# DMA transposes in place of TensorE transposes, chunks of 128 and 97 rows, and warming matmuls, in an attention plus Fourier-mix plus feed-forward kernel

## The chip, the cores and the metric

One core of one Trainium2 chip. The time is device microseconds of a whole launch; lower is better. The kernel before took 689.9 us (median of three runs, 689.3 to 690.1). Engines: PE is TensorE, DVE VectorE, ACT ScalarE, POOL GpSimd, SP the engine that issues most DMAs here. The kernel's matmuls write to PSUM tiles (`psS`, `psF`, `psT`); the copy out of one by VectorE or ScalarE is called its evacuation.

## The reference

Eight batches of 448 rows, 12 heads of 64, width 768:

```
attn  = relu(q @ k^T / 8)^2 / 448
x     = heads_to_rows(attn @ v)                     # (8, 448, 768)
u     = x + real(fft(fft(x, axis=1), axis=2))
un    = (u - mean(u)) / sqrt(var(u) + 1e-6)         # per row
out   = u + relu(un @ w1) @ w2                      # w1 768x3072, w2 3072x768
```

The two Fourier transforms are matmuls with cosine and sine tables ("mix"). By symmetry only half of the rows is computed, and the lower half comes out mirrored.

Of the kernel before, what the change touches and what calls it, by code (L numbers as in the profile page):

```python
# [9 lines left out]
FP32 = mybir.dt.float32  # L10
# [32 lines left out]
class Streams:  # L43
# [8 lines left out]
    def dma(self, start, nbytes):  # L52
        self.dma_free = max(self.dma_free, start + 1.0) + nbytes / 400e3
        return self.dma_free + 1.2
# [60 lines left out]
def kernel(  # L115
# [14 lines left out]
    R1 = R + 1  # L130
    NS = S // 2 + 1
    NQ = 2 * NS
# [6 lines left out]
    SC = [(0, R), (R, NS)]  # L139
    XB = 2  # L140
# [8 lines left out]
    HS = S // 2  # L149
    utop = [dram.tile([HS, D], FP32, name=f"utop{b}") for b in range(B)]  # L150
    ubot = [dram.tile([HS + 1, D], FP32, name=f"ubot{b}") for b in range(B)]

# [19 lines left out]
    rev = const.tile([128, R], BF16, name="rev")  # L172

    back = [const.tile([R, 1], mybir.dt.int32, name=f"back{i}") for i in range(2)]
    qT_bufs = []
# [5 lines left out]
    def dft_indices():  # L181
        nc.gpsimd.iota(drow[:, 0:2], pattern=[[R, 2]], base=0, channel_multiplier=1,
                       allow_small_or_imprecise_dtypes=True)
        nc.gpsimd.iota(drow[:, 4:7], pattern=[[128, 3]], base=0, channel_multiplier=1,
                       allow_small_or_imprecise_dtypes=True)
        nc.gpsimd.iota(dcol[:, 0:NS], pattern=[[1, NS]], base=0, channel_multiplier=0,
                       allow_small_or_imprecise_dtypes=True)
        nc.gpsimd.iota(dcol2, pattern=[[1, 2], [2, KH]], base=0, channel_multiplier=0,
                       allow_small_or_imprecise_dtypes=True)

    def small_constants():
        nc.vector.memset(zero_t, 0.0)
        nc.vector.memset(eps_t, 1e-6)
        for i in range(3):
            t = const.tile([128, NQ], BF16, name=f"qT{i}")
            nc.vector.memset(t[:, NS:NS + 1], 0.0)
            nc.vector.memset(t[:, NQ - 1:NQ], 0.0)
            qT_bufs.append(t)

    def mirrors():  # L200
        nc.gpsimd.memset(rev, 0.0)
        nc.gpsimd.affine_select(out=rev, in_=rev, compare_op=ALU.not_equal, fill=1.0,
                                base=1 - R, pattern=[[1, R]], channel_multiplier=1)
        for i in range(2):
            nc.gpsimd.iota(back[i], pattern=[[0, 1]], base=(2 - i) * R, channel_multiplier=-1)

    seq = const.tile([R1, 2, 2, NS], BF16, name="seqm")
# [3 lines left out]
    def build_dft():  # L211
# [16 lines left out]
        for t in range(2):  # L228
            e = yield need("DVE", 0.5)
            y = work.tile([128, 4 * KH], FP32, name="dfty", tag="u", bufs=2)  # L230
            for i in range(2):
                nc.vector.tensor_scalar(y[:R1, i * NS:(i + 1) * NS], col[:R1, 0:NS],
                                        row[:R1, i:i + 1], 0.25 if t == 0 else 0.0,
                                        op0=ALU.mult, op1=ALU.add)
            yield from sincos(seq[:, t, :, :].rearrange("p a s -> p (a s)"), y, 2 * NS, R1)
# [17 lines left out]
    BQ = [Bufs(3) for _ in range(3)]  # L253

    def load_group(i):
# [3 lines left out]
        for x, (nm, src) in enumerate((("q", q), ("k", k), ("v", v))):  # L259
            e = yield need("POOL", 0.85, bufs=[BQ[x]])  # L260
            t = work.tile([R, 2 * HG, 2 * Dh], BF16, name=f"{nm}n", tag=f"{nm}n", bufs=3)
# [3 lines left out]
            ready[i][x].t = sch.dma(e, GRP)  # L265
# [7 lines left out]
            if i == 1 and x == 2:  # L273
                yield need("POOL", 0.7)
                mirrors()

# [39 lines left out]
    xTs, As, Bs = [[] for _ in range(B)], [[] for _ in range(B)], [[] for _ in range(B)]  # L316
# [4 lines left out]
    BQR, BQT, BKT = Bufs(2), Bufs(3), Bufs(2)  # L321
    turned = [[None] * MC for _ in range(B)]
    turned_at = [[Cell() for _ in range(MC)] for _ in range(B)]

    def turning():
        for b in range(B):
            for m in range(MC):
                g, h0 = divmod(2 * m, HG)
                if h0 == 0:

                    qk = []
                    for x in range(2):
                        e = yield need("DVE", 0.42, [ready[b * NG + g][x]], [BQR] if x == 0 else [])
                        o = work.tile([R, 4, HG, Dh], BF16, name="qkr", tag=f"qkr{x}", bufs=2)
                        nc.vector.tensor_copy(o, loads[b * NG + g][x])  # L335
                        BQ[x].free.append(e)
                        qk.append(o.rearrange("p c h d -> p c (h d)"))

                hs = slice(h0 * Dh, (h0 + 2) * Dh)
                early = b == 0  # L340
                e = yield need("PE", 8 * 0.055, [e + LATENCY["DVE"]], [BF if early else BT])
                pt = psF(BF16) if early else psT(BF16)
                for c in range(4):
                    for x in range(2):
                        nc.tensor.transpose(pt[:, x * S + c * R:x * S + (c + 1) * R],  # L345
                                            qk[x][:, c, hs], ident[:R, :R])
                if h0 > 0:
                    BQR.free.append(e)
                e1 = yield need("DVE", 0.85, [e + LATENCY["PE"]], [BQT])
                qT = qT_bufs[(b * MC + m) % 3]  # L350

                nc.vector.tensor_copy(qT[:, 0:2 * R].rearrange("p (r j) -> p r j", j=2),  # L352
                                      pt[:, 0:2 * R].rearrange("p (j r) -> p r j", j=2))
                nc.vector.tensor_copy(qT[:, NS + 1:NS + 2 * R - 1].rearrange("p (r j) -> p r j", j=2),
                                      pt[:, 2 * R:4 * R].rearrange("p (j r) -> p r j", j=2)[:, :0:-1, ::-1])

                nc.vector.tensor_copy(qT[:, 2 * R:4 * R + 1:2 * R], pt[:, 2 * R:4 * R:R])
                e2 = yield need("ACT", act(S), [e + LATENCY["PE"]], [BKT])
                kT = work.tile([128, S], BF16, name="kT", tag="kT", bufs=2)
                nc.scalar.activation(kT, pt[:, S:2 * S], AF.Copy)  # L360
                (BF if early else BT).free.append(max(e1, e2))
                turned[b][m] = qT, kT
                turned_at[b][m].t = max(e1, e2) + LATENCY["ACT"]

    def attention(b):
# [4 lines left out]
        for p in range(NP + 2):  # L370
            m, c0 = divmod(p * G, 4)
            deps, bufs, dur = [], [], 0.0
            if p < NP:
                deps.append(turned_at[b][m])
                bufs += [BS] * G
                dur += G * mm(NQ) + SWITCH
            if p >= 2:
# [6 lines left out]
                dur += G * mm(NQ) + SWITCH  # L384
# [3 lines left out]
            if p < NP:  # L388
                qT, kT = turned[b][m]
                for c in range(c0, c0 + G):  # L390
                    sc = psS()
                    for h in range(2):
                        ps = slice(h * Dh, (h + 1) * Dh)
                        nc.tensor.matmul(sc[:R, h, 0:NQ], lhsT=kT[ps, c * R:(c + 1) * R], rhs=qT[ps, :],  # L394
                                         start=True, stop=True)
                    scs.append(sc)
                if c0 + G == 4:
                    BQT.free.append(e)
                    BKT.free.append(e)
            av_end = None  # L400
            if p >= 2:
# [3 lines left out]
                for c in range(ca, ca + G):  # L405
                    sq = sqs.pop(4 * ma + c)[0]
                    for h in range(2):
                        nc.tensor.matmul(av[h * Dh:(h + 1) * Dh, 0:NQ], lhsT=vn[:, c, h0 + h, :],  # L408
# [7 lines left out]
            for i in sorted(relus):  # L416
                r, t = relus.pop(i)
                e1 = yield need("DVE", dve2(2 * NQ), [t], [BSQ])
                sq = work.tile([R, 2, NQ], BF16, name="sq", tag="sq", bufs=4)
# [3 lines left out]
            for i, sc in enumerate(scs):  # L423
                e1 = yield need("ACT", act(2 * NQ) - 0.03, [e - dur * 0.5 + LATENCY["PE"]], [BAR])
                r = work.tile([R, 2, NQ], BF16, name="rsc", tag="rsc", bufs=2)
                nc.scalar.activation(r, sc[:R, :, 0:NQ], AF.Relu)  # L426
                BS.free.append(e1 + 0.1)
                relus[p * G + i] = (r, e1 + LATENCY["ACT"])
            if av_end is not None:
                m2 = ma  # L430
                e1 = yield need("DVE", dve(NQ) + 2 * dve2(NS), [av_end],
                                [BX[m2]] + ([BA[m2]] if m2 < 3 else []))
                x = work.tile([128, NQ], BF16, name="xT", tag=f"xT{m2}", bufs=1)
                nc.vector.tensor_scalar(x, av[:, 0:NQ], 1.0 / (64.0 * S), None, op0=ALU.mult)  # L434
                BT.free.append(e1 - 2 * dve2(NS))
                xTs[b].append(x)
                x_ready[b][m2].t = e1
                f = work.tile([128, 2, NS], BF16, name="fold", tag=f"fold{min(m2, 3)}", bufs=1)
                nc.vector.tensor_tensor(f[:, 0, :], x[:, 0:NS], x[:, NS:NQ], op=ALU.add)
                nc.vector.tensor_tensor(f[:, 1, :], x[:, 0:NS], x[:, NS:NQ], op=ALU.subtract)  # L440
                F.append(f)
                if m2 >= 3:
                    i = m2 - 3
                    e1 = yield need("DVE", 2 * dve2(NQ))
                    t = work.tile([128, 2, NS], BF16, name="diff", tag=f"diff{i}", bufs=1)
                    nc.vector.tensor_tensor(t, F[i], f, op=ALU.subtract)
                    Bs[b].append(t)
                    nc.vector.tensor_tensor(F[i], F[i], f, op=ALU.add)
                    As[b].append(F[i])
                    ab_ready[b][i].t = e1 + LATENCY["DVE"]  # L450
# [5 lines left out]
    BXN = [Bufs(XB), Bufs(XB)]  # L456
# [4 lines left out]
    u_stored = [[Cell() for _ in range(4)] for _ in range(B)]  # L461
    un_ready = [[Cell() for _ in range(2)] for _ in range(B)]
    uns = [[None] * 4 for _ in range(B)]
    groups, tails = [], []

    def mix_rows(b, ch, pcs):
# [3 lines left out]
        xT = xTs[b]  # L470
        xs = []
        for i in range(2):

            e = yield need("PE", 6 * 0.06, x_ready[b], [BT])
            px = psT(BF16)
            c0 = i * NS + s0
            for m in range(MC):
# [288 lines left out]
```

## The kernel before: what the change touches

The feed-forward of a pair of batches is cut into one group of 384 rows (feed-forwards 0, 2, 4, 6; "even") and one of 512 rows (1, 3, 5, 7; "odd"); feed-forwards are numbered from 0 here. While feed-forward *b* runs, TensorE does, in gaps chosen by a list scheduler in the program, attention of the next two batches and the mix of batch *b+1*. The scheduler fixes the order of instructions on every engine when the kernel is built; on the chip each engine then takes them in that order. One constant says how early attention may run, in units of one feed-forward:

```python
    LEAD = 1.6
    ...
            lead = b + p / NP - LEAD        # p: step of the attention of batch b
            e = yield need("PE", dur + SWITCH, deps, bufs, lambda: progress[0] >= lead)
```

All transposes are matmuls against an identity. Queries and keys (q/k):

```python
                    for x in range(2):
                        nc.tensor.transpose(pt[:, x * S + c * R:x * S + (c + 1) * R],
                                            qk[x][:, c, hs], ident[:R, :R])
                # ... three VectorE copies build qT, one ScalarE copy builds kT
```

The attention result is made as x^T and turned back into rows for `u`, six transposes for each of four row blocks; then the rows are normalised on VectorE, and `un` is turned for the feed-forward:

```python
            for m in range(MC):
                nc.tensor.transpose(px[:n, m * 128:(m + 1) * 128], xT[m][:, c0:c0 + n], ident)
            nc.scalar.activation(x[:n], px[:n, 0:D], AF.Copy)
            # ... mix, u, statistics ...
            nc.vector.tensor_scalar(un[:n], u[:n], rstd[:n, i:i + 1], nmr[:n, i:i + 1],
                                    op0=ALU.mult, op1=ALU.add)
            # ... per 256 columns:
                    nc.tensor.matmul(pu[:, h, c0:c0 + w], lhsT=uns[b][t][:n, ms], rhs=idn, ...)
            nc.scalar.activation(dst[...], pu[:, :, c0:c1], AF.Copy)     # unT
```

## Time and profile before

| | before |
|---|---|
| span of the profiled run | 686.8 us |
| first feed-forward matmul | 90.14 us |
| third to fifth feed-forward (two batches) | 155.40 us |
| TensorE busy in those two batches | 153.74 us |

The third row is the yardstick. The first matmul of each feed-forward is easy to find in the timeline of TensorE (the first one that reads `unT` after the last that reads `hT`), and from the third to the fifth (2 to 4) the kernel is in its steady rhythm: one group of 384 and one of 512 rows, with attention and mix of two batches in between. Here it is as a line of the windows table of the kernel before (stretch in us, its length, then busy time and number of instructions of PE, PEld, DVE, ACT and POOL, granted clock, DMA share, GB/s):

```profile
249.79:405.19 155.40, 153.74 (x1069) 83.76 (x1072) 94.25 (x219) 86.47 (x137) 28.11 (x31) 1.00 0.44 80
```

TensorE idles 1.66 us in 155.40. What is taken from TensorE here can be gained; a new wait of TensorE is paid in full.

### The profile page before, as it was taken

How to read it: one execution, taken by the hardware profiler on the slowest of the kernel's cores; microseconds unless marked ns; L12 is line 12 of the kernel's file. 1: busy time of each engine (PE TensorE's matmuls, PEld its weight loads, DVE VectorE, ACT ScalarE, POOL GpSimd, SP SyncE). 2: the span in 40 equal slices, each digit the busy share in tenths (PEclk: the TensorE clock that was granted, in tenths of full speed). 3: DMA queues.
4: the chain of work that ended last, by engine and by line, in shares of the span. 5: the costliest groups of instructions: out<-in, count | busy, mean ns of one | idle time of the engine just before them, and what ended most of it. 6: DMA issues, size and time to landing. Idle time of an engine off the chain costs nothing.

```text
span 686.8 us, 10715 instructions
## 1 busy us (share of the span) xinstructions
PE 640.7 (93%) x4270; PEld 347.9 (51%) x4288; DVE 388.1 (57%) x902; ACT 354.9 (52%) x556; POOL 126.3 (18%) x154
## 2 busy tenths in 40 slices
PE   2777399999999999999999999999999999999997
PEld 1235245654447545664446545664446545664464
DVE  7765956396545865396545964386545944280011
ACT  3755377527655466526755467426755367414400
POOL 8313321131112211131102111122101200030000
PEclk9999589999999999999999999999999999999999
DMA  9996994436315464435325464435232420042011
GB/s 125 212 167 109 225 151 41 41 130 125 32 17 94 141 110 42 41 130 118 34 20 82 154 111 42 41 129 111 26 36 41 150 89 1 1 151 69 1 70 69
DMA packets 82178, 59.70 MB, mean 87 GB/s; under 512 B 67528, under 2 KB 70600, under 8 KB 82128
## 3 DMA queue, kind: packets, MB, share of 16 engines
q0 software_dynamic: 71808, 31.46, 34.5%
q1 hardware_dynamic: 10320, 27.56, 12.1%
q8 instruction: 33, 0.54, 0.3%
q14 instruction: 17, 0.14, 0.1%
HBM read 62.91 MB, written 22.04 MB: 124 GB/s over the span
## 4 chain that ended last, share of the span: by engine, by line
PE 67%; DVE 19%; ACT 5%; DMA 4%; issue 2%; POOL 2%; ACTq 0%; DVEq 0%; POOLq 0%
PE psF L678 32%; PE psF L713 18%; PE psT L408 5%; PE psS L394 5%; DVE stats L522 4%; ACT rsc L426 3%; DVE un L536 3%; PE psS L573 3%; DVE sq L420 2%; DVE o L695 2%; PE psT L345 2%; DMA kn<-in_k_dram 2%; DMA w<-in_moe_w_ch_dram 2%; DVE u L512 2%; PE psT L478 1%
## 5 line engine op out<-in xcount | busy, mean ns | idle before, releaser
L426 ACT ACTIVATE rsc<-psS 112x900 bf16<-112x900 f32 x192 | 174.6, 921 | 132.9 <-PE psS L394 72.7
L678 PE MATMUL psF<-unT,w 128*128 128x384 bf16 (+1 forms) x1134 | 231.5, 354 | 2.5 <-ACT hT L668 1.4
L713 PE MATMUL psF<-w,hT 128*128 128x384 bf16 x1344 | 231.6, 326 | 0.0
L713 PEld LDWEIGHTS <-hT 128*128 128x128 bf16 x1344 | 127.0, 98 | 91.9 <-issue 14.0
L678 PEld LDWEIGHTS <-w 128*128 128x128 bf16 x1152 | 107.6, 98 | 113.7 <-issue 23.3
L668 ACT ACTIVATE hT<-psF 128x384 bf16<-128x384 f32 (+1 forms) x192 | 104.2, 545 | 61.1 <-PE psF L678 60.9
L420 DVE TENSOR_TENSOR sq<-rsc 112x900 bf16<-112x900 bf16 x192 | 114.0, 621 | 37.8 <-ACT rsc L426 35.7
L394 PE MATMUL psS<-qT,kT 64*112 64x450 bf16 x384 | 67.6, 413 | 14.1 <-ACT rsc L426 7.3
L695 DVE TENSOR_TENSOR o<-psF,o 128x384 f32<-128x384 f32 x56 | 30.7, 548 | 76.8 <-PE psF L713 76.7
L408 PE MATMUL psT<-sq,vn 112*64 112x450 bf16 x384 | 63.1, 398 | 11.1 <-DVE sq L420 10.7
L434 DVE TENSOR_SCALAR xT<-psT 128x450 bf16<-128x450 f32 x48 | 30.0, 625 | 75.5 <-PE psT L408 75.3
L262 POOL DMA_DIRECT2D vn<-in_v_dram x24 | 20.9, 871 | 268.0 <-PE psT L408 267.0
L394 PEld LDWEIGHTS <-kT 64*112 64x112 bf16 x384 | 21.9, 132 | 50.3 <-issue 43.9
L352 DVE COPY qT<-psT 128x224 bf16<-128x224 bf16 x42 | 16.4, 391 | 49.7 <-PE psT L345 49.3
L511 POOL TENSOR_TENSOR u<-tp,xn 112x385 f32<-112x385 f32 (+1 forms) x16 | 14.9, 934 | 149.6 <-DVE tp L502 128.6
L408 PEld LDWEIGHTS <-vn 112*64 112x64 bf16 x384 | 16.3, 111 | 47.3 <-issue 44.4
L345 PEld LDWEIGHTS <-qkr 112*128 112x128 bf16 x384 | 25.5, 107 | 18.0 <-DVE qkr L335 11.6
L522 DVE BATCH_NORM_STATS2 stats<-u 112x6 f32<-112x384 f32 (+1 forms) x64 | 31.6, 534 | 0.0
L526 ACT ACTIVATE std<-mv,eps_t 112x2 f32<-112x2 f32 (+1 forms) x16 | 4.7, 296 | 50.5 <-DVE mv L523 50.5
L536 DVE TENSOR_SCALAR un<-u,rstd,nmr 112x768 bf16<-112x768 f32 (+1 forms) x32 | 28.3, 915 | 0.6
L484 ACT ACTIVATE xn<-psT 112x768 bf16<-112x768 bf16 (+1 forms) x32 | 25.3, 812 | 6.5 <-PE psT L478 6.5
L586 DVE CAST pc<-psS 112x384 bf16<-112x384 f32 (+1 forms) x16 | 9.5, 594 | 32.0 <-ACT pc L584 32.0
(72 smaller groups left out, 498.1 us busy)
## 6 DMA issues: line engine op xcount, KB each, us to landing
out_dram<-o SPq DMA_DIRECT2D x28, 384.0 KB
qn<-in_q_dram POOLq DMA_DIRECT2D x24, 224.0 KB, 5.3
kn<-in_k_dram POOLq DMA_DIRECT2D x24, 224.0 KB, 5.8
vn<-in_v_dram POOLq DMA_DIRECT2D x24, 224.0 KB, 4.3
utop<-u SPq DMA_DIRECT2D x16, 336.0 KB
w<-in_moe_w_ch_dram POOLq DMA_DIRECT2D x12, 384.0 KB, 13.7
w<-in_moe_w_ch_dram POOLq DMA_DIRECT2D x4, 1152.0 KB, 17.7
o<-utop SPq DMA_DIRECT2D x8, 384.0 KB
```

What stands on the lines that cost most here:

```text
L345: nc.tensor.transpose(pt[:, x * S + c * R:x * S + (c + 1) * R], qk[x][:, c, hs], ident[:R, :R])
L394: nc.tensor.matmul(sc[:R, h, 0:NQ], lhsT=kT[ps, c * R:(c + 1) * R], rhs=qT[ps, :], start=True, stop=True)
L408: nc.tensor.matmul(av[h * Dh:(h + 1) * Dh, 0:NQ], lhsT=vn[:, c, h0 + h, :], rhs=sq[:, h, :], start=(c == 0), stop=(c == 3))
L420: nc.vector.tensor_tensor(sq, r, r, op=ALU.mult)
L426: nc.scalar.activation(r, sc[:R, :, 0:NQ], AF.Relu)
L434: nc.vector.tensor_scalar(x, av[:, 0:NQ], 1.0 / (64.0 * S), None, op0=ALU.mult)
L522: nc.vector.bn_stats(stats[:n, hf, :], u[:n, hf * (D // 2):(hf + 1) * (D // 2)])
L536: nc.vector.tensor_scalar(un[:n], u[:n], rstd[:n, i:i + 1], nmr[:n, i:i + 1], op0=ALU.mult, op1=ALU.add)
L668: nc.scalar.activation(h[:, 0:N], ph[:, 0:N], AF.Relu)
L678: nc.tensor.matmul(ph[:, 0:N], lhsT=w1_sb[m][hf][:, jj * 128:(jj + 1) * 128], rhs=unT[:, m, 0:N], start=(m == 0), stop=(m == MC - 1))
L695: nc.vector.tensor_tensor(o[:, hs], pc[:, 0:D // 2], o[:, hs], op=ALU.add)
L713: nc.tensor.matmul(pc[:, 0:D // 2], lhsT=hT[j][:, c * 128:(c + 1) * 128], rhs=w2_sb[j // 6][:, j % 6, hs], start=(j == 0), stop=(j == JC - 1))
```

## The change

Its intent is to take the transposes off TensorE and their evacuations off ScalarE and VectorE, and to have the DMA engines, busy 44% of the time, do them. Batch 0 keeps TensorE transposes for q/k and for all but the last 64 rows of un, as there is nothing to hide a DMA behind. Core of the diff, cuts marked (the scheduler's `need` lines are mostly left out; so are fewer buffers, two for three, for the loaded q and k, and one for two for their reordered copies):

```diff
-    SC = [(0, R), (R, NS)]                 # row chunks 112 + 113
+    SC = [(0, 128), (128, NS)]             # 128 + 97
...
+                        nc.sync.dma_start_transpose(out=t, in_=qk[x])              # q, k
...
+        nc.sync.dma_start_transpose(out=xns[b][:, :, m * 128:(m + 1) * 128], in_=xTc[m])
...
-            nc.vector.tensor_scalar(un[:n], u[:n], rstd[:n, i:i + 1], nmr[:n, i:i + 1],
-                                    op0=ALU.mult, op1=ALU.add)
+            nc.scalar.activation(un[:n], u[:n], AF.Identity, bias=nmr[:n, i:i + 1],
+                                 scale=rstd[:n, i:i + 1])
...
+    def store_rows(ch, top, bot, us, nbytes, t, cells):     # for u (fp32) and for un (bf16)
...
+            nc.sync.dma_start(out=top[s0:s0 + w, :], in_=us[0][:w])
+        if ch == 1:
+            nc.sync.dma_start(out=bot[0:1, :], in_=us[1][w:w + 1])
+        nc.gpsimd.indirect_dma_start(               # the mirrored lower half
+            out=bot, out_offset=bass.IndirectOffsetOnAxis(ap=back[ch][:w], axis=0),
+            in_=us[1][:w], in_offset=None)
...
+            # turn_un: two or three of these a batch, from the DRAM tensors ntop and nbot
+            nc.sync.dma_start_transpose(out=g[:, :, c0:c0 + w], in_=src[r0:r0 + w, :])
...
+    def warming():
+        while progress[0] == 0.0:                   # until the first feed-forward
+            e = yield need("PE", 0.12 if e > 5.0 else 0.23)
+            nc.tensor.matmul(pw[:, 0:256], lhsT=warm[:, 0:128], rhs=warm, start=True, stop=True)
...
+        sch.add(warming(), (9, 9))                  # last priority in the scheduler
```

So from batch 1 on `un` goes out to DRAM, its lower half by an indirect scatter that mirrors it, and comes back transposed.

## The prediction

> **What bounds the kernel now.** I read the page's busy row and its 40 slices first, then a table of three stretches cut where those slices change, then the chain of waits, and last the timeline of TensorE at single places, for the price of one transpose.
>
> ```profile
> PE 640.7 (93%) x4270; PEld 347.9 (51%) x4288; DVE 388.1 (57%) x902; ACT 354.9 (52%) x556; POOL 126.3 (18%) x154
> PE   2777399999999999999999999999999999999997
> PEclk9999589999999999999999999999999999999999
> ```
> ```profile
> 0.00:90.00 90.00, 53.69 (x296) 27.45 (x296) 65.88 (x165) 49.13 (x68) 35.91 (x55) 0.90 1.11 168
> 90.00:650.00 560.00, 554.36 (x3778) 301.17 (x3795) 317.71 (x730) 304.62 (x487) 90.35 (x99) 1.00 0.39 75
> 650.00:687.00 37.00, 32.67 (x199) 19.28 (x197) 4.46 (x8) 1.19 (x2) 0.00 (x0) 0.99 0.18 64
> ```
> The columns are the stretch in us, its length, the busy time of PE, PEld, DVE, ACT and POOL, the granted clock, the DMA share and GB/s. There are two kernels in one. From 90 us on (the first feed-forward matmul is at 90.21) TensorE is busy 554.4 of 560 us at full clock, while VectorE has 57% and the DMA engines 39%. There the time is the sum of TensorE's slots, and only 5.6 us are idle. Before 90 us TensorE idles 36 us, and VectorE (65.9 of 90) carries the chain, with the clock down to 0.59 between 68 and 90 us. So TensorE work taken out after 90 us should come off one for one, if nothing new makes TensorE wait; work taken out before counts only if it lies on the VectorE chain.
>
> The chain of waits for the whole span says the same, two thirds TensorE:
> ```profile
> PE 67%; DVE 19%; ACT 5%; DMA 4%; issue 2%; POOL 2%; ACTq 0%; DVEq 0%; POOLq 0%
> ```
>
> Now the price of a transpose. The mean in the group table (222 ns) includes the pipeline; the start-to-start distance in the timeline is what a slot costs. Columns: start, length, engine, line, operation, shapes.
> ```profile
> 290.04 0.83 PE L478 MATMUL psT<-ident,xT 128*112 128x128 bf16 x12
> 290.71 1.14 PE L713 MATMUL psF<-w,hT 128*128 128x384 bf16 x6
> ...
> 301.64 0.59 PE L394 MATMUL psS<-qT,kT 64*112 64x450 bf16 x4
> 302.16 0.57 PE L408 MATMUL psT<-sq,vn 112*64 112x450 bf16 x4
> 302.67 7.00 PE L713 MATMUL psF<-w,hT 128*128 128x384 bf16 x42
> ...
> 323.25 0.56 PE L345 MATMUL psT<-ident,qkr 112*128 112x112 bf16 x8
> 323.65 1.46 PE L678 MATMUL psF<-unT,w 128*128 128x512 bf16 x6
> ```
> Eight q/k transposes take 323.65 - 323.25 = 0.40 us, 0.050 each; twelve of x^T 0.67 us, 0.056 each. Four score and four value matmuls take 302.67 - 301.64 = 1.03 us, 0.129 each. The eight un transposes at 312.63 to 313.04 (next fence) take 0.41 us, 0.051 each.
>
> The place that decides this case is the boundary between two batches:
> ```profile
> 312.63 0.27 PE L616 MATMUL psS<-ident,un 112*128 112x112 bf16 x2
> ...
> 313.04 0.56 PE L345 MATMUL psT<-ident,qkr 112*128 112x112 bf16 x8
> ...
> 316.94 2.77 PE L678 MATMUL psF<-unT,w 128*128 128x512 bf16 x11
> ```
> ```profile
> 294.08 0.55 DVE L502 TENSOR_TENSOR tm<-psS,qs 112x385 f32<-112x385 f32 x1
> 309.55 1.27 DVE L536 TENSOR_SCALAR un<-u,rstd,nmr 113x768 bf16<-113x768 f32 x2
> ```
> The normalised rows are complete at 310.8 us, TensorE turns them from 312.6, and the next feed-forward starts at 316.9. That is almost no slack: the latency from the mix to the feed-forward is just hidden.
>
> **What the Trainium skill says.** "VectorE: DVE Perf Modes", section "The three transpose paths", gives 390 ns for one 128x128 transpose on TensorE and 1309 ns by DMA. This trace's 50 to 56 ns slot is the pipelined price of the former; no run here yet shows a DMA transpose. "DMA: Bandwidth & Descriptors", "Latency and other measured facts", gives a DMA transpose an effective 261 GB/s, also not shown yet. The same page, "Two DMAs through the same engine are not ordered", says a DMA that reads what another wrote must wait for that one's completion. The trace agrees in kind: the second indirect scatter to ubot waits 4.8 us for an earlier DMA to the same tensor, and a scatter takes 4.7 us from issue to landing. "TensorE: Matmul & The Clock Gate", Part 1, says the clock halves after about 3.4 us without work; the 0.59 at 68 to 90 us (TensorE busy 10.7 of 22) fits, though the first 17 us, busy 4.5, show 1.00.
>
> **The change part by part.**
>
> 1. TensorE work removed. q/k transposes: 336 of 384 (batch 0 keeps PE). x^T: all 192. un: 168 of 192. In the old program order 88 + 24 + 24 of these stand before the first feed-forward matmul, so after it the old kernel has 296 x 0.050 = 14.8, 168 x 0.056 = 9.4, 168 x 0.051 = 8.6, together 32.8 us. In the other direction, 20 score and 12 value matmuls of batch 1 that the old kernel did before the first feed-forward now come after it: 32 x 0.129 = 4.1 us. Net -28.7 us on a path where TensorE is the bound. The 450 to 448 columns and chunks of 128 and 97 rows change almost nothing: the moving size stays.
>
> 2. The old boundary wait. At 312.6 to 317.0 TensorE is busy 3.4 of 4.4 us, held by the evacuation of unT on ScalarE; that goes for seven batches. Of the 5.6 us idle I count -4.
>
> 3. VectorE and ScalarE. VectorE loses the three qT copies (0.39 + 0.38 + 0.17 = 0.94 us, six per batch) and un (four of 0.9); it gains a second xT copy, perhaps 0.15 each. About -8 us per batch. ScalarE loses kT (6 x 0.54), xn (4 x 0.81) and unT (3 x 0.9), gains un (4 x 0.8): about -6. Neither bounds after 90 us, so this only shortens the mix chain.
>
> 4. The start. In the old chain the mix of batch 0 runs from 61.5 to 90.2 us. Its 24 matmuls took 3.9 us at the low clock and need about 2.0 warm (-1.9). The stretch from the last un to the feed-forward, 84.35 to 90.21, holds 1.6 us of batch-1 transposes and attention plus cold un transposes (-2.4). Batch-1 squares and one relu on the chain go (-2.5), un moves off VectorE (-1), and the first feed-forward matmuls run warm (-1). Before that, batch 1's qT copies leave VectorE's queue (-2). Sum about -10 to -11; I take -10, as the 516 warming matmuls stand in TensorE's in-order queue and may delay a real one now and then. First feed-forward at about 80 us.
>
> 5. The new latency. From batch 1 on, un is no longer turned in 4 us by TensorE. It is stored to DRAM, its lower half scattered after a one-row store to the same tensor, then read back transposed in two or three DMAs, each waiting on the one before. Estimate: the row store 2.4, the scatter 4.7, the transpose about 3.5 including its issue (an estimate from 344 KB at the skill's 261 GB/s, 1.3 us, and fixed latency), about 10.5 us. The chain from the second mix matmul to the last un was 19 us in the old trace (291.7 to 310.8) and should be about 16 with less on VectorE: 26 to 27 in all, about 25 for batch 7, where attention no longer competes. Against this stands what the new order gives TensorE between that matmul and the next feed-forward, at the slots above: 32, 31 and 31 us for batches 2, 4, 6; but 21, 24 and 24 for 1, 3, 5, and 20 for 7. Waits: 0 for even batches, and 5.5 + 3 + 3 + 5.5 = 17 us for the odd ones. The order itself betrays it: before feed-forwards 1, 3 and 5 three or four score/value groups stand back to back, which ScalarE feeds at about 1.8 us a group (two relus of 0.92) against 1.03 on TensorE.
>
> Sum: -10 - 28.7 - 4 + 17 = -26, so 689.9 - 26 = about 664; I say 663.
>
> **The rivals.** (a) The new latency is hidden: waits of about 3 us in place of 17, time about 648. For it: VectorE is lighter and both row chunks of the mix are issued together. Against it: batch 7 has nothing left to fill with. (b) The latency is worse: DMA transposes queue on the one in-order SP queue behind output stores that wait for VectorE, or land late, so q/k turns late as well. At 10 us per batch rather than 17 in all: about 695. Against it: q/k groups are double buffered a third of a batch ahead, some 25 us. (c) DMA becomes the bound. The transposes move 9.6 (q/k) + 6.3 (x^T) + 4.9 (un) = 20.8 MB, 80 us at 261 GB/s, on engines now busy 47% of 687 us, 323 us: 403 of 660, 61%. Not a bound unless they run at a third of that rate. In the start, where the share is already at its ceiling (1.11), they may cost a few us. (d) Warming does nothing but delay: lose 3 to 4 of the 10 us at the start, about 667.
>
> **Range and chances.** The TensorE saving is nearly certain in size; the waits at four to seven boundaries are not, from 3 to 35 us, and the start is worth +-4. Range 645 to 682. Faster by over 2% means below 676.1: 0.82. Within 2%: 0.15. Slower: 0.03.
>
> **What would show it.** In the changed profile: first feed-forward at 77 to 83 us with the clock at 9 throughout (step 4); TensorE's real work after it about 29 us less (step 1); idle gaps of 3 to 6 us ahead of feed-forwards 1, 3, 5, 7, put down to a DMA into unT, and none ahead of 2, 4, 6 (step 5); DMA share around 0.6. Wrong would be: waits on qkT or xn in mid-batch, gaps ahead of every feed-forward, or a first feed-forward no earlier than 88 us.

## The result

The changed kernel took 723.1 us (720.2 to 725.9, four runs), against 689.6 us for the kernel before on the same chip. The ratio is 1.0485, 95% interval 1.043 to 1.054: slower by almost 5%, where 4% faster had been predicted. (A ratio is the mean time of one kernel's fast runs over that of the other's in the same rounds, so not quite the ratio of the medians quoted.)

The page of the changed kernel, the same rows that the prediction showed of before, and its chain of waits:

```profile
PE 659.9 (92%) x4109; PEld 352.8 (49%) x4109; DVE 339.9 (47%) x779; ACT 327.8 (46%) x481; POOL 138.3 (19%) x173
PE   8999999885999899995999899994999899977997
PEclk9999999996999899996999999995999999998999
...
PE 81%; DVE 9%; DMA 5%; issue 2%; ACT 1%; SPq 1%; POOL 0%; DVEq 0%; POOLq 0%; ACTq 0%
```

TensorE is "busy" 19 us longer than before, but 64 of its 660 us are the 517 warming matmuls. The new thing is in the slices: at places where before had an unbroken row of nines there are dents (5, 5, 4, 7), and under each the clock dips as well. A DMA has 5% of the chain. The yardstick, from the windows table of the changed kernel:

```profile
261.55:422.83 161.28, 148.76 (x882) 74.35 (x880) 81.33 (x187) 78.89 (x117) 32.44 (x34) 0.95 0.70 122
```

There are 187 fewer TensorE instructions than before, but TensorE now idles 161.28 - 148.76 = 12.5 us and runs at 0.95 of its clock. The waits table of TensorE says for whom (line waited for: total us, times, longest):

```profile
PE psF L712 <- DMA unT<-nbot: 24.6, 3, 9.6
PE psS L441 <- ACT rsc L473: 16.3, 18, 2.9
```

The first is the feed-forward waiting for the transposed rows; a fourth such wait, 8.7 us at the last batch, is put down to "issue". The second is a score matmul waiting for a relu on ScalarE. All of both lies after the first feed-forward matmul; the kernel before has no wait of either kind there (its 7.3 us of waits for relus all lie in the start). Three places carry the whole result.

**The start.** From the timeline of the changed kernel, all engines:

```profile
61.24 23.63 PE L765 MATMUL psF<-warm 128*128 128x256 bf16 x215
...
73.49 1.95 ACT L549 ACTIVATE un<-u,nmr,rstd 97x768 bf16<-97x768 f32 x2 [0.43 <-DVE nmr L544]
...
87.68 0.49 PE L712 MATMUL psF<-unT,w 128*128 128x384 bf16 x2
```

The rows of batch 0 are normalised at 75.4 us, but TensorE still has warming matmuls in its queue until about 84.7 us, and only then turns the rows. The scheduler had placed 215 of them in that gap at an estimated 0.12 us each; the estimate of the gap was too long.

**The odd boundaries.** The boundary ahead of feed-forward 3, the same view:

```profile
316.87 1.94 ACT L549 ACTIVATE un<-u,nmr,rstd 97x768 bf16<-97x768 f32 x2
317.06 1.16 POOL L569 DMA_INDIRECT nbot<-un,back  x1 [0.30 <-ACT rsc L473]
...
320.37 0.25 SPq L567 DMA_DIRECT2D nbot<-un  x1
...
322.31 0.91 POOL L569 DMA_INDIRECT nbot<-un,back  x1 [4.08 <-ACT rsc L473]
...
323.76 0.88 POOL L265 DMA_DIRECT2D vn<-in_v_dram  x1 [0.54 <-PE psT L455]
...
326.21 1.32 SPq L734 DMA_DIRECT2D out_dram<-o  x1
327.64 3.16 SPq L592 DMA_TRANSPOSE unT<-nbot  x1
...
336.06 1.04 PE L712 MATMUL psF<-unT,w 128*128 128x512 bf16 x2 [6.94 <-DMA unT<-nbot]
```

Read it as a relay. Scatter of chunk 0, one-row store, scatter of chunk 1 and read-back all touch `nbot`, so each waits for the one before. The last one waits for a queue as well: the second scatter landed 3.9 us after its issue, at 326.2, but by then an output store (326.21) stood ahead of the read-back in SP's queue and held it 1.4 us more. The relay of `u` ahead of this one has a like effect: the `un` of chunk 0 was complete at 312.6, but its scatter stood 4.5 us in GpSimd's queue, behind a scatter of `u` that waited 3.7 us for the one-row store to `ubot`. `un` is complete at 318.8; the row store goes out 1.6 us later, the second scatter 1.9 us after that, the read-back 5.3 us after the scatter, and it lands 8.4 us later: 17.3 us from `un` to the matmul. The name in brackets on the second scatter (a relu on ScalarE) is only the semaphore that came last by the profile; `un` had long been there, and it was the row store that held it, as the run without row stores shows below.

**The middle of the odd feed-forwards.** The same view again, in feed-forward 1, 23 us ahead of feed-forward 2, while the mix of batch 2 is under way:

```profile
237.32 0.30 ACT L539 ACTIVATE std<-mv,eps_t 97x2 f32<-97x2 f32 x1 [1.79 <-DVE mv L536]
237.87 0.92 ACT L473 ACTIVATE rsc<-psS 112x896 bf16<-112x896 f32 x1 [0.25 <-DVE rstd L542]
...
238.84 0.62 PE L441 MATMUL psS<-qkT 64*112 64x448 bf16 x2 [2.86 <-ACT rsc L473]
...
240.28 5.25 PE L747 MATMUL psF<-w,hT 128*128 128x384 bf16 x18
```

TensorE waits 2.86 us for a score buffer. The relu that frees it stands in ScalarE's queue behind `std` of the second row chunk, which itself waits for statistics on VectorE; the two `un` of the first chunk, now on ScalarE, fill the same queue shortly before (1.95 us from 232.43). The 18 matmuls that follow take 5.25 us; 18 of the same matmuls take 3.09 us at full clock (in e8). In that stretch the granted clock was 0.57. So the wait costs twice.

The predicted TensorE saving is there all the same: the odd feed-forwards, 88.25 us before, take 86.7 to 88.7 with this wait and the low clock in them. How large it is shows where these are taken away (e2).

### The profile page after: what moved, and what is told of

The parts are those of the page before. It is cut to its first block, busy times and chain, and to the rows that moved or that the text cites. A ratio compares the mean times of both kernels' runs of the same rounds, so it can differ in the third digit from the quotient of the medians.

```text
span 719.3 us, 10591 instructions
## 1 busy us (share of the span) xinstructions
PE 659.9 (92%) x4109; PEld 352.8 (49%) x4109; DVE 339.9 (47%) x779; ACT 327.8 (46%) x481; POOL 138.3 (19%) x173
## 4 chain that ended last, share of the span: by engine, by line
PE 81%; DVE 9%; DMA 5%; issue 2%; ACT 1%; SPq 1%; POOL 0%; DVEq 0%; POOLq 0%; ACTq 0%
PE psF L712 32%; PE psF L747 25%; PE psF L765 7%; PE psS L441 6%; PE psT L455 6%; DMA unT<-nbot 4%; PE psS L618 2%; DVE stats L535 2%; PE psS L502 1%; DVE u L524 1%; DVE sq L467 1%; ACT rsc L473 1%; DVE o L729 1%; DVE u L523 1%; DMA unT<-ntop 1%
## 5 line engine op out<-in xcount | busy, mean ns | idle before, releaser
L712 PE MATMUL psF<-unT,w 128*128 128x512 bf16 (+1 forms) x1152 | 233.7, 360 | 33.4 <-DMA unT<-nbot 24.6
L473 ACT ACTIVATE rsc<-psS 112x896 bf16<-112x896 f32 x192 | 170.5, 916 | 124.7 <-PE psS L441 93.2
L712 PEld LDWEIGHTS <-w 128*128 128x128 bf16 x1152 | 110.9, 99 | 153.3 <-issue 52.7
L467 DVE TENSOR_TENSOR sq<-rsc 112x896 bf16<-112x896 bf16 x192 | 114.8, 619 | 87.9 <-ACT rsc L473 87.6
L441 PE MATMUL psS<-qkT 64*112 64x448 bf16 x384 | 63.7, 381 | 17.3 <-ACT rsc L473 16.3
L765 PE MATMUL psF<-warm 128*128 128x256 bf16 x517 | 64.3, 279 | 1.1 <-DVE warm L195 1.1
L455 PE MATMUL psT<-sq,vn 112*64 112x448 bf16 x384 | 59.6, 381 | 0.0
L765 PEld LDWEIGHTS <-warm 128*128 128x128 bf16 x517 | 49.6, 100 | 12.2 <-issue 4.6
L441 PEld LDWEIGHTS <-qkT 64*112 64x112 bf16 x384 | 21.2, 125 | 54.6 <-issue 53.5
L549 ACT ACTIVATE un<-u,nmr,rstd 128x768 bf16<-128x768 f32 (+1 forms) x32 | 31.1, 1018 | 15.3 <-DVE nmr L544 15.3
L535 DVE BATCH_NORM_STATS2 stats<-u 128x6 f32<-128x384 f32 (+1 forms) x64 | 31.9, 539 | 0.0
L339 DVE COPY qkr<-kn 112x1024 bf16<-112x1024 bf16 x24 | 10.1, 422 | 32.0 <-DMA qkT<-qkr 32.0
```

The costliest lines, as they stand in the source:

```text
L441: nc.tensor.matmul(sc[:R, h, 0:S].rearrange("k (c q) -> k c q", c=4), lhsT=kT[ps, m % 2, c, :], rhs=qT[ps, m % 2], start=True, stop=True)
L455: nc.tensor.matmul(av[h * Dh:(h + 1) * Dh, 0:S], lhsT=vn[:, c, h0 + h, :], rhs=sq[:, h, :], start=(c == 0), stop=(c == 3))
L467: nc.vector.tensor_tensor(sq, r, r, op=ALU.mult)
L473: nc.scalar.activation(r, sc[:R, :, 0:S], AF.Relu)
L535: nc.vector.bn_stats(stats[:n, hf, :], u[:n, hf * (D // 2):(hf + 1) * (D // 2)])
L549: nc.scalar.activation(un[:n], u[:n], AF.Identity, bias=nmr[:n, i:i + 1], scale=rstd[:n, i:i + 1])
```

## The experiments

The table lists all runs; the edits follow. "Two batches" is the yardstick (before 155.4, changed kernel 161.3), "first" the first feed-forward matmul. Times are medians; the kernel before took 688.6 to 689.0 us beside the experiments and 689.6 beside the changed kernel, whose four runs spread over 6 us, so differences to it are good to about 3.5 us, half the width of the interval above. All ran on one chip but for e15, which has its own kernel before beside it.

| run | us | ratio to before (95%) | first, us | two batches, us |
|---|---|---|---|---|
| changed kernel | 723.1 | 1.049 (1.043-1.054) | 87.7 | 161.3 |
| e1 99 warming matmuls less | 713.5 | 1.036 (1.034-1.038) | 77.6 | 162.5 |
| e11 no warming | 714.4 | 1.039 (1.036-1.042) | 75.6 | 161.0 |
| e2 LEAD 1.8 | 672.8 | 0.978 (0.976-0.980) | 87.7 | 145.2 |
| e6 no one-row stores (wrong rows) | 695.3 | 1.012 (1.008-1.016) | 87.7 | 153.6 |
| e4 scatters of 97 rows | 811.8 | 1.178 (1.176-1.180) | 87.7 | 185.8 |
| e3 rows on TensorE | 685.8 | 0.994 (0.991-0.998) | 88.7 | 153.8 |
| e5 e3 + un on VectorE | 673.2 | 0.977 (0.976-0.979) | 89.2 | 149.4 |
| e10 e5 without warming | 667.7 | 0.970 (0.968-0.973) | 77.0 | 149.4 |
| e12 e10 + q/k on TensorE | 677.6 | 0.985 (0.982-0.988) | 87.0 | 153.3 |
| e7 e1 + e2 + rows of batch 1 on TensorE | 661.0 | 0.961 (0.958-0.964) | 77.6 | 146.4 |
| **e8 e7 without warming** | **655.3** | **0.951 (0.950-0.953)** | 76.1 | 145.8 |
| e9 e8 + un on VectorE | 670.8 | 0.974 (0.971-0.978) | 76.7 | 150.2 |
| e13 before + LEAD 1.8 | 703.0 | 1.021 (1.018-1.024) | 90.5 | 158.4 |
| e14 e10 + LEAD 1.8 | 675.4 | 0.980 (0.977-0.983) | 76.6 | 150.4 |
| e15 e8 + rows on TensorE | 668.0 | 0.972 (0.969-0.974) | 76.4 | 149.1 |

My theory after the result was that the 17 us of boundary waits had been under-sized and that the warming blocked the start. The first rival: it is the DMA transposes as such (q/k and x^T late too). The second: un on ScalarE.

**e1, fewer warming matmuls.** The scheduler's clock still counts them, so that no other order changes:

```diff
-            nc.tensor.matmul(pw[:, 0:256], ...)
+            if not 400 <= i < 499:
+                nc.tensor.matmul(pw[:, 0:256], ...)
```

> The changed kernel with 99 of the 215 warming matmuls between the mix of batch 0 and its un transposes left out, nothing else. Theory (warming blocks TensorE's in-order queue: un was ready at 75.4 us, TensorE came to it at 84.7): first feed-forward at about 78.5 us in place of 87.7, time 723 - 9 = 714, the waits ahead of feed-forwards 1, 3, 5, 7 as before. Rival (the start is set by something else, the DMA loads for instance): 721 to 725.

It took 713.5 us. The timeline of e1:

```profile
61.22 12.83 PE L766 MATMUL psF<-warm 128*128 128x256 bf16 x116
...
77.58 0.65 PE L712 MATMUL psF<-unT,w 128*128 128x384 bf16 x3
```

The feed-forward starts 10.1 us earlier, and by the medians 9.6 us of it reach the end. The blocking is shown.

**e2, attention earlier.** One constant:

```diff
-    LEAD = 1.6
+    LEAD = 1.8
```

> The changed kernel with LEAD 1.8 for 1.6: attention and mix of batches 2 to 7 come a fifth of a feed-forward earlier in TensorE's order, so 36 us at the nominal slots stand between mix and feed-forward for 3 and 5, and 30 for 7, in place of 24 and 20; batch 1 stays. Theory (the wait is latency of the store, scatter and read-back chain, 29 to 35 us from mix to rows, and nothing else): waits ahead of 3 and 5 gone, of 7 nearly, that of 1 unchanged, about 40 us off, 683. Rival (DMA engines or the SP queue are too full, so that the chain grows with whatever is put in front of it, or q/k and x^T come late): above 700.

It took 672.8 us, 50 less where 40 were expected. The yardstick and the wait, from the windows and waits tables of e2:

```profile
260.11:405.26 145.15, 143.61 (x877) 72.74 (x880) 80.76 (x186) 77.75 (x116) 32.35 (x34) 1.00 0.79 135
```
```profile
PE psF L712 <- DMA unT<-nbot: 8.8, 2, 8.5
```

The work is the same (877 and 882 TensorE instructions), the idle time fell from 12.5 to 1.5 us, and the busy time from 148.8 to 143.6 with the clock back at 1.00. So 16 us of two batches were 11 us of waiting and 5 us of slow clock after the waits. The waiting is of both kinds: in the whole run that for the transposed rows fell from 33.3 to 8.8 us, and that of scores for relus from 16.3 to 5.4, though un stayed on ScalarE. Earlier attention also lets the mix come earlier: 36.9 us lie between the start of the last mix matmuls and feed-forward 3 (287.50 to 324.40), all of it filled with work, where the changed kernel had 35.1 us with 6.9 of them empty. The DMA share is 0.79, so the DMA engines bear more per microsecond than before the edit and bound nothing. Only the boundary ahead of feed-forward 1 still waits, 8.5 us.

**e13, the same constant in the kernel before.** This is the control: would the old kernel have gained as well? (The edit is the same line.)

> The kernel before with the attention allowed earlier (the constant LEAD from 1.6 to 1.8), nothing else. Theory, that this constant paid in the changed kernel only because it hid the round trip of the rows through DRAM: there is no such trip here, so 689 within 4 us, and two feed-forwards from the third to the fifth still take 155 us. Rival, that the earlier attention is a gain of its own: 675 to 680, and those two take under 152 us.

It took 703.0 us, 14 us *more* than with 1.6, which neither view had said. From the waits table of e13:

```profile
PE psS L394 <- ACT rsc L426: 17.7, 12, 3.6
```

With 1.6 this line is 7.3 us, all of it in the start; so in the kernel before, where un does not travel through DRAM, attention further ahead adds 10.4 us of score matmuls waiting for relus. The 50 us of e2 are therefore no gain that was lying about: of these two values, the old kernel is faster with the old one and the changed kernel with the new one, and it was shipped with the old one. One doubt remains, as the change also moved un to ScalarE: from e3 to e15 below (both with the rows on TensorE and un on ScalarE) LEAD 1.8 and no warming win 17.8 us, and leaving out the warming was worth only 5.5 to 8.7 elsewhere. So some 9 to 12 of the 50 us may be a better order for un on ScalarE and not a hidden round trip; no run changes LEAD alone in that kernel.

**e6, a shorter relay.** Row 0 of each `ubot` and `nbot` is zeroed at the start and the one-row stores are dropped. Its output is wrong, which doesn't matter for the time.

```diff
-        if ch == 1:
-            e = yield need("SP", 0.1, [t[1]])
-            nc.sync.dma_start(out=bot[0:1, :], in_=us[1][w:w + 1])
```

> The changed kernel (723.1 us) with row 0 of every ubot and nbot written once at the start with zeros, so without the one-row store between the two scatters; wrong on purpose in one row of 448 per batch. Theory (scatter, row store, scatter to one DRAM tensor are serial, and the wait for the row store of u also holds the GpSimd queue): 4 to 5 us off at each of four boundaries, about 704. Rival (the read-back transpose, 8 us in a busy queue, is what counts and moves with the rest): 716 or more.

It took 695.3 us, 28 less where 19 were expected. The boundary ahead of feed-forward 3, from the timeline of e6:

```profile
308.47 1.93 ACT L556 ACTIVATE un<-u,nmr,rstd 97x768 bf16<-97x768 f32 x2
310.68 0.97 POOL L573 DMA_INDIRECT nbot<-un,back  x1 [4.80 <-ACT un L556]
...
314.10 1.73 SPq L596 DMA_TRANSPOSE unT<-nbot  x1
...
318.48 0.61 PE L716 MATMUL psF<-unT,w 128*128 128x512 bf16 x1
```

The second scatter leaves 0.3 us after `un` is done (310.4) in place of 3.5, and the feed-forward follows after 8.1 us in place of 17.3. Of the 9.2 us won here, 3.2 are the one-row store of 1.5 KB that held the second scatter, 1.9 the way from there to the next issue, and 4.0 the read-back, which lands within 4.4 us of its issue where it took 8.4. The excess over the expected gain fits that last part, which I had not expected to move; what the traces show of it stands below, under what stays open.

**e4, the row scattered too.** The index list would take 97 rows as well as 96, so the one-row store can go without a wrong result:

```diff
-        if ch == 1:
-            nc.sync.dma_start(out=bot[0:1, :], in_=us[1][w:w + 1])
+        w += ch
```

> The changed kernel without the one-row stores: row 0 of the lower half goes as the 97th row of the second chunk's indirect scatter, for u and for un. Theory (the chain of three dependent DMAs to one DRAM tensor, scatter, row store, scatter, is a large part of the 17 us between un and the feed-forward): some 5 us off at each of four boundaries, about 703. Rival (the transposed read-back in a busy DMA queue is the long part, 8.4 us of it measured): 718 or more.

This was the largest miss: 811.8 us, and TensorE waits 112.7 us for `unT`. The list of DMA issues (count, median us from issue to landing), first of the changed kernel, then of e4:

```profile
nbot<-un,back POOLq DMA_INDIRECT x15, 4.1
```
```profile
nbot<-un,back POOLq DMA_INDIRECT x15, 16.3
```

One row more in every second scatter, and the median over all of them (those of 128 rows share the queue) goes up four times. The Trainium skill, "DMA: Bandwidth & Descriptors", section "Why a DMA increments its semaphore by 16 and not by 1", states that the number of DMA engines which share a transfer is the largest number up to 16 that divides the sizes of the slowest dimension, with one exception for some direct copies: 96 partitions get 16, and 127 get one. 97 is a prime. The records of single DMA packets in the two packed traces agree. In the changed kernel the 96-row scatter of `un` at boundary 3 is 32 packets of 4.6 KB, up to 16 of them at once, all done within 1.1 us; in e4 the 97-row one is the same 32 and a short one, strictly one after another, over 7.5 us.

**e3, rows on TensorE.** The round trip of `un` is taken out altogether: `un` is turned by matmuls as before, q/k and x^T stay with the DMA.

```diff
-        if b > 0:
-            yield from turn_un(b)
-            return
+        # every batch: 24 transposes on TensorE, ScalarE writes unT
```

> The changed kernel with the normalised rows turned on TensorE for all batches (as before the change), no nbot and ntop; q/k and x^T still by DMA, warming as it is. Theory (the round trip of un through DRAM is what costs; q/k and x^T by DMA are hidden): all four long waits go, 8.6 us of TensorE transposes and some 4 us of evacuation waits come back, 723 - 58 + 12 = about 677. Rival (DMA transposes of q/k and x^T also make TensorE wait, or slow it): above 700.

It took 685.8 us, 37 less than the changed kernel, yet 9 more than expected. In the yardstick the even feed-forward took 63.6 us, 3.6 less than before, but the odd one needed 90.3, 2 more than before, at a clock of 0.96. The timeline showed the 2.85 us wait of the third place above, at 384.85 us, with no DMA of rows left to blame. That was not in my theory; it gave the next experiment.

**e5, e3 with un on VectorE.**

```diff
-            nc.scalar.activation(un[:n], u[:n], AF.Identity, bias=nmr[...], scale=rstd[...])
+            nc.vector.tensor_scalar(un[:n], u[:n], rstd[...], nmr[...], op0=ALU.mult, op1=ALU.add)
```

> The kernel of e3 (rows turned on TensorE for all batches, 685.8 us) with the normalisation of un back on VectorE. In e3 TensorE waited 2.9 us for an attention relu in each even-to-odd feed-forward and then ran at low clock. Theory (un on ScalarE stands in its in-order queue ahead of the attention relus and waits there for VectorE; 3.3 us idle and 2 to 3 us of low clock in each of feed-forwards 1, 3, 5): these waits go, 686 - 17 = about 669. Rival (those waits come from VectorE's own load or from the DMA, and un on VectorE adds its 3.6 us per batch there): 684 or more.

673.2 us: the longest wait of a score matmul for a relu falls from 2.9 to 0.6 us, the odd feed-forward from 90.3 to 84.9 us at clock 1.00. As the scheduler sees the other engine it also picks another order for the attention steps, so the 12.6 us are the engine and the order together.

**e7 to e9, the best version and two doubts.** e7 joins LEAD 1.8, the cut of e1 and, for the one boundary that e2 left, rows of batch 1 on TensorE.

> All mends together: LEAD 1.8, 99 warming matmuls left out, the rows of batch 1 turned on TensorE (the one boundary that the lead cannot widen), the rest by DMA as changed. Theory (three separate costs that add: warming 9 us, the wait ahead of feed-forward 1 some 16 us, the others gone with the lead): 672.8 - 9.5 - 15 = about 648. Rival (what is taken away at one place comes back at the next): above 660.

It took 661.0 us, 13 more than expected, which is what the rival said: the first feed-forward and what lies in it became 10.2 us shorter than in e2, but the second 6.3 us longer (91.5 against 85.2), with 510 TensorE instructions in it rather than 484: work that had stood ahead of the wait now comes after it. e8 is e7 without `sch.add(warming(), (9, 9))`.

> The kernel of e7 with no warming matmuls at all. Theory (warming does speed the mix of batch 0 and the first feed-forward matmuls, by 1.9 + 1 to 2 us, once it does not block): e7 plus 3 to 5 us, about 652. Rival (warming is of no use at all, and its instructions still delay attention of batch 0): equal to e7 or up to 3 us faster.

The rival was right in direction, and the gain was larger than the 3 us it allowed: 655.3 us, 5.7 faster than with warming (3.2 in the two profiled runs), and the fastest correct kernel. The page and the timeline of e8:

```profile
PE 604.0 (92%) x3600; PEld 306.8 (47%) x3616; DVE 339.0 (52%) x779; ACT 327.2 (50%) x484; POOL 136.7 (21%) x171
```
```profile
58.81 2.41 PE L502 MATMUL psS<-pc,seqm 97*128 97x385 bf16 x7 [0.99 <-DVE pc L631]
...
76.07 4.19 PE L721 MATMUL psF<-unT,w 128*128 128x384 bf16 x14
```

Without warming the seven mix matmuls take 2.41 us rather than the 1.32 of e7, but nothing stands in front of the real work, and the feed-forward starts 1.5 us earlier. e9 puts un on VectorE in e8, as had paid in e5.

> The kernel of e8 (655.3 us) with un back on VectorE. Theory (what e5 showed, un on ScalarE holding up attention's relus, still costs something in the early feed-forwards 0 to 2, where the lead gives no slack): 2 to 5 us off, about 652. Rival (with the longer lead nobody waits for those relus any more, and VectorE's extra 3.6 us per batch lengthens the mix instead): 655 to 658.

It took 670.8 us: a miss of 19 and the reverse of e5. The timeline of e9:

```profile
281.27 1.75 DVE L549 TENSOR_SCALAR un<-u,rstd,nmr 128x768 bf16<-128x768 f32 x2
...
286.64 0.57 DVE L467 TENSOR_TENSOR sq<-rsc 112x896 bf16<-112x896 bf16 x1
286.75 0.30 ACT L539 ACTIVATE std<-mv,eps_t 97x2 f32<-97x2 f32 x1 [7.10 <-DVE mv L536]
...
291.81 3.68 PE L756 MATMUL psF<-w,hT 128*128 128x384 bf16 x12
```

Now un and the statistics of the second chunk stand ahead of the attention's squares on VectorE; ScalarE waits 7.1 us at `std` with the relus behind it; TensorE waits 1.3 and 2.0 us for scores and runs the next 12 matmuls in 3.68 us, where 2.12 is the full-clock time. It is the third place again, with the engines exchanged. The even feed-forwards 2 and 4 take 69.6 and 70.0 us, against 64.3 in e8.

**e10, e11, e12: what each part is worth.** e10 is e5 without warming, e11 the changed kernel without it, e12 turns q/k of all batches on TensorE in e10 (`if b > 0:` becomes `if False:`, and from batch 1 on they use the PSUM buffers that the kernel before used), so that only x^T is left to the DMA.

> The kernel of e5 (673.2 us) without the warming matmuls, so the change reduced to its q/k and x^T transposes by DMA and the chunks of 128 and 97 rows. Theory (warming costs as in e8, some 12 us over the old start): 673 - 12 = 661. Rival (without warming the mix of batch 0 runs cold and gives it back): 668 or more.

> The changed kernel (723.1 us) without the warming matmuls, nothing else. Theory (they cost more than the 9.6 us that e1 took back, as e8 was 5.7 us faster than e7): 708 to 711. Rival (the gain of e8 was of that kernel alone): 713 as e1, or more.

> The kernel of e10 with q and k of all batches turned on TensorE again, so x^T by DMA alone is left of the change. Theory (a transpose taken off TensorE in the steady part is worth its slot, 296 x 0.050 = 14.8 us for q/k): e10 plus 15, about 676. Rival (the q/k transposes are worth less, since their DMA adds waits, or more, since their evacuations go as well): e10 plus under 10, or over 20.

e10 took 667.7 us and e11 714.4: the rivals were right both times (e10 within 0.3 us), removing all of the warming is worth 5.5 us in one and, in the other, the same as removing a fifth of it. In none of the three pairs did it help. e12 took 677.6 us, near the 676 expected, but that was taken from an e10 seven microseconds faster: against the measured e10 it is 9.9 us more, not 15, so the rival's "under 10" is what was met, if barely.

**e14 and e15: the rows alone.** e14 is e10 with LEAD 1.8; e15 is e8 with the rows on TensorE, as in e3.

> Queries, keys and x^T by DMA, normalised rows on TensorE with un on VectorE, no warming, and LEAD 1.8: the comparison of e10 (LEAD 1.6, 667.7 us) and of e8 (rows by DMA, LEAD 1.8, 655.3 us). Theory: without a round trip LEAD moves nothing, 668 within 3 us, so the rows by DMA are worth 12 us once hidden (some 4 us in two feed-forwards, 149.4 here against 145.8). Rival: LEAD itself made the difference between e10 and e8, then 655 to 660.

> The fastest kernel (e8) with the normalised rows of batches 2 to 7 turned on TensorE again; un stays on ScalarE, LEAD 1.8 and no warming. It differs from e8 in the rows alone. Theory: once hidden, the rows by DMA save their transposes and evacuations, 24 x 0.051 = 1.2 us of TensorE a batch and some short waits: 4 us in two feed-forwards (150 against 145.8) and 10 to 12 in all, 667. Rival, as e14 showed for un on VectorE (its two feed-forwards took 150.4 against 150.2 of e9, whichever way the rows were turned): the order of the queues decides and the rows are worth nothing, 655 to 658.

e14 took 675.4 us, 8 *more* than e10, and neither view had that. As in e9, un on VectorE and LEAD 1.8 do not go together: the even feed-forwards 2 and 4 take 69.6 to 71.6 us in both, against 64.5 in e10. In its source e15 differs from e8 in the rows alone (the scheduler orders the rest anew), and it took 668.0, as the theory said. With the latency hidden, the rows by DMA are worth 12.7 us; with LEAD 1.6 they cost 37 (e3 against the changed kernel).

## Why the prediction was wrong

Said: 663 us, 645 to 682. Measured: 723.1. By the prediction's own steps:

1. **TensorE work removed: right in size.** For two batches its own slots give 96 x 0.050 + 48 x 0.056 + 48 x 0.051 = 9.9 us. TensorE's busy time in the yardstick fell from 153.74 to 143.61 us, 10.1, once the clock was undisturbed (e2). By parts, from the table: x^T with the new chunks 155.4 - 153.3 = 2.1 (predicted 2.7), q/k 153.3 - 149.4 = 3.9 (4.8), rows 149.1 - 145.8 = 3.3 (2.4).
2. **The old boundary wait:** at most the 1.7 us of idling in the yardstick's two batches could go; it stayed, at 1.5 in e2. A gain of 4 us in all was a little too much.
3. **"Neither bounds after 90 us, so this only shortens the mix chain": failed.** The count of busy time was right (VectorE and ScalarE are lighter), but moving un changed what stands ahead of the attention's relus in ScalarE's in-order queue. The 16.3 us of waits of scores for relus, none of which the old kernel had after its first feed-forward, and the low clock after them, go with that. (An un of 128 rows also took 1.0 us on ScalarE, not 0.8.) Step 5 does end with the remark that ScalarE feeds back-to-back score groups more slowly than TensorE takes them, but the sum counted nothing for it. Taking un off ScalarE again, with the order that then results, is worth 12.6 us (e3 to e5); in another order of the attention it costs 15.5 (e8 to e9), and the order of e2 leaves only 5.4 us of these waits with un still on ScalarE. So the engine alone does not decide it; the order that goes with it does too.
4. **The start: the chain right, the warming wrong.** Un of batch 0 was complete at 75.4 us, so a start at 77 to 80 was there to be had, and e1 and e8 have it (77.6 and 76.1). The step gave the warming a loss "now and then"; it cost 9.6 us in one piece. The sign that the prediction had named for being wrong, a first feed-forward no earlier than 88 us, was met but for 0.3 us. (The 90.21 us that it gives for the old kernel's first feed-forward matmul is 90.14 in the trace; nothing rests on it.)
5. **The new latency: failed in size, and decided the case with what followed from it.** Direction, place and cause were named (odd boundaries, the relay through DRAM, too little work to fill). Its two sums were mis-sized. From un to the feed-forward it said 10.5 us and 17.3 was measured: row store (2.4 said, 1.9 measured) and scatter (4.7 said, 5.3 with the way to the next issue) were nearly right, but the read-back took 8.4 us instead of 3.5, and 1.6 us went to the wait of the row store for the first scatter, which was not on the list. From mix to un, 16 was said and 17.9 measured. So the chain took 35.1 us, not 26 to 27, at boundary 3, and what stood in front of it filled 28.2, not 24; the waits were 8.0, 6.9, 9.6 and 8.7 us, 33 in all, not 17.
6. **What no step had:** the slow clock that goes with the waits. Around boundary 3 it was 0.50 from 326.6 to 340.3 us, so from the waits of scores just ahead of the boundary on. At boundary 3 the first 24 feed-forward matmuls took 7.41 us, against 5.36 for 24 of them at full clock (in e7). In two batches this made 5 us (e2).

Of the rivals, (b), worse latency, and (d), warming that only delays, came true together, and each beyond its number. Of the two reasons that (b) gives, output stores in the SP queue show at boundary 3 with 1.4 us; that q/k turns late does not show, as no matmul of the changed kernel waits for a q/k transpose by DMA. (c), the DMA as the bound, is refuted: a share of 0.80 in e8 goes with the fastest time. (By its own sum the limit would lie at a quarter of the rate, 323 + 4 x 80 = 643 of 660 us, not at a third.) (a), hidden latency at 648, is what e8 comes close to with 655.

The sum, by start and rest of the span (686.8 before, 719.3 after): the start gave -2.5 us in place of -10; the rest +35 in place of -28.7 - 4 + 17 = -15.7. The 58 us of error are 8 of warming and 51 of waits and slow clock, and e2, which leaves all transposes in place, wins 50 of the latter back. The windows of the rest split the 51. TensorE's idle time rose from 9.8 to 55.9 us, by 46 where steps 2 and 5 allow 13: of the 33 too much, 16 are the boundaries (33 us, not 17), and about 17 are chiefly the waits for relus that step 3 ruled out. Its busy time fell by 11.1 us where step 1 has 28.7; the 18 between are mostly slow clock, since in e2 it fell by 25.4.

What stays open: why the read-back takes 8.4 us at boundary 3 and at most 4.4 in e6. The traces point to the loads of the next q, k and v. At boundaries 1, 3 and 5 of the changed kernel these three DMAs are issued just before or beside the read-back (at boundary 3 from 323.76 us on), and it takes 9.0, 8.4 and 9.7 us from issue to the matmul; at boundary 7 there is nothing left to load, and it takes 4.0, close to the 3.5 of the prediction. In e6 they come after the read-back at boundary 3. The DMA engines were busier in that stretch of the changed kernel (share 1.51 against 1.08). All this fits, but no run moves the loads alone.

## What to carry to other kernels

Moving work from a saturated engine to an idle one by way of DRAM buys throughput and sells latency: before counting the saving, lay the whole relay (every store and every transfer on the same tensor, in the order issued) beside the work that can stand in front of it, and retune the constant that sets this distance; here it was worth 50 us in the new kernel (not all of it by hiding the relay) and cost 14 in the old. When an operation changes its engine, ask what stands behind it in that engine's queue, not how busy the engine is. Filler work in an in-order queue needs a measured gap, and a row count that is one off a good number can cost more than the row saves.

## What the Trainium skill lacked or had wrong

- "DMA: Bandwidth & Descriptors", "Latency and other measured facts", gives a DMA transpose a bandwidth only. The estimate from it (3.5 us with issue) met 7.8 us as the median of the eleven read-backs from `nbot` and 8.4 us at boundary 3. At boundary 7, with no loads beside it, one took 4.0 us. The median landing was 3.1 us for q/k and 4.6 us for x^T. No page that I drew on has a latency for a transpose beside other traffic; the 1309 ns that the prediction quotes is for a single 128x128 block.
- The same page has no time for issuing a transpose on SP of this chip, only cycle counts beside its part on trn3. In these traces one holds the issuing engine 1.2 to 1.5 us as a rule, 3.2 us at boundary 3 (327.64) and up to 5.0 at boundary 5, against 0.25 to 0.4 for most plain DMAs.
- The same page, "Why a DMA increments its semaphore by 16 and not by 1", states its rule and, for some direct copies, an exception; it does not name the indirect scatter. The rule held for it here: packets of a 96-row scatter ran up to 16 at once (1.1 us), those of a 97-row one singly (7.5 us), and the median of all these scatters to landing rose from 4.1 to 16.3 us.
- "VectorE: DVE Perf Modes", "The three transpose paths", gives 390 ns for a TensorE transpose. In a pipelined row the slot is 50 to 56 ns here, and taking 192 of them out of two batches saved 10.1 us, 53 ns each. For choosing a path it is the slot that counts, and that table does not give it; the page of the next point has a start-to-start time for matmuls in general.
- "TensorE: Matmul & The Clock Gate", Part 1, puts the loss of clock after about 3.4 us without work. Here a wait of 2.86 us, with 0.44 us shortly before it, was followed by a clock of 0.57 over 5 us, so 3.4 us wholly without work were not needed: in the 3.4 us up to 237.9, where the clock fell, TensorE was busy 1.04. And keeping TensorE warm did not pay: without warming the kernel was 5.7 us faster (e8 against e7), though its first mix matmuls ran at 2.41 us in place of 1.32.
